# Loading q in long rows, turning it per residue, and keeping TensorE busy during the first loads

## The chip, the cores and the metric

The kernel runs on one NeuronCore of a Trainium2 chip. The metric is the device time of one execution in microseconds (us), as the median of several runs.

## The reference

Two stages follow one another. The first is attention with a decay per head, over 4 batches of 8 heads, 768 positions and 64 dimensions, in blocks of 64 positions with a running state:

```python
for b in range(nb):
    intra = einsum('bhic,bhjc->bhij', qb, kb) * Dmask      # lam ** (i - j) for i >= j
    intra = einsum('bhij,bhjd->bhid', intra, vb)
    inter = einsum('bhid,bhde->bhie', qb * lam_pow, kv_state)
    out[:, :, sl] = intra + inter
    kv_state = lam_block * kv_state + einsum('bhsd,bhse->bhde', kb * rev_pow, vb)
```

The second takes that output as x (4 batches, 768 positions, 512 features) through a mixer over positions and one over features, in float32:

```python
h = relu(x.transpose(0, 2, 1) @ w_tok1) @ w_tok2
u = x + h.transpose(0, 2, 1)
out = u + relu(u @ w_ch1) @ w_ch2
```

## The kernel before

The attention runs over 16 pairs: pair i is one batch and two heads (h = 0, 1), whose 2 x 64 dimensions fill the 128 partitions. The 768 positions stand in six chunks c of 128. Block length in the kernel is the chunk of 128, with the mask and the powers of lam computed on chip for it.

All engines run their instructions in the order in which the program issues them (a manual schedule), so the order of the Python code is the order of each engine's queue. A loop goes over i from -2 to 15, and one turn of it works on several pairs:

- `scores(i + 1)` (L304): for each half g of three chunks, 6 matmuls give k times q into two banks of PSUM; VectorE (DVE) multiplies them by the mask into `a` (L312). `scale_q` (L257, GpSimd, here POOL) multiplies q by powers of lam.
- `outputs(i, g)` (L328 and L338): the weights `a` times v and the scaled q times the state, into `xT`; ScalarE (ACT) copies it to `uT` (L345).
- `state(i + 1)` (L270): k times v per chunk into `kv`, which DVE scans into `sv` with the factors in `keep` (L278). `place`, later, has POOL copy `sv` into `stb` (L291).
- `masks(i + 2)` (L179, for the first four pairs): DVE builds two heads' masks by a scan over the identity.
- the turns of pair i + 2: positions must become the free axis of `kT` and `qT`. For pairs under `NKD` = 8 `turn_k` has TensorE (PE) turn the chunks with the identity into a bank of PSUM, three chunks to a half g, and ACT copies it out (L220, L225). For pairs under `NQ` = 5 `turn_q_rows` does the same for q (L241, L242). Later pairs come by loads of 128-byte rows (`load_dims`, L115) and DVE's 32x32 transposes (L230, L234).
- `turn_back` (L360, L368, L369): the finished `uT` is turned for the mixer and split into a high and a low part.
- `scale_k(i + 2)` (L250 on ACT, L252 on POOL): k times the decay, into `kd`.
- loads, on SyncE's queue (SP): `load_v(i + 3)` (L157), `load_kq(i + 4)` (L137 for k, L140 for q).

Between these steps the code puts work of the mixer over positions: `load_w1` (L407) brings w_tok1 in three parts, and `convert_w1(i)` queues for each part a few steps on DVE, ACT and POOL (L388 to L397, L379, L380), which are taken out one by one during the next turn of the loop. From pair 4 on matmuls with these weights (L456, L493) fill PE beside the attention. After the attention, from about 140 us on, comes the mixer over features.

Before the loop `load_first` loads k of pair 0 from SP and q of pair 0 from ACT, each in four pieces; then v and k, q of the next pairs. `make_identity` builds `ident` on POOL. DVE builds `mask` of the first pair and, by repeated doubling, `lamp` (L198, L201), the powers of lam; POOL copies from it into `keep` for all four pairs of heads (L206). The turns of PE share three banks of PSUM (`bank("sh", ...)`); `xT` has one bank of its own.

As q is loaded before, partition s of the tile holds positions s, s + 128, s + 256 and so on: one piece of 256 bytes for each chunk and head.

Of the kernel before, what the change touches and what calls it, by code (L numbers as in the profile page):

```python
# [9 lines left out]
F32 = mybir.dt.float32  # L10
# [12 lines left out]
def kernel(  # L23
# [23 lines left out]
    nc = tc.nc  # L47
    B, H, S, D = q.shape
# [3 lines left out]
    P = 128  # L52
    NC = S // P
    NH = NC // 2
    NP = H // 2
# [48 lines left out]
    NQ = 5  # L104
    NKD = 8
    loaded = {}
# [3 lines left out]
    def load_dims(to, src, b, p):  # L110
        for h in range(2):
            sv = src[b, 2 * p + h].rearrange("(blk s) (di d) -> di s blk d", s=32, di=2)
            for di in range(2):
# [2 lines left out]
                    out=to[n * 32 : (n + 1) * 32].rearrange("p (blk d) -> p blk d", d=32), in_=sv[di]  # L116
                )

    def load_first():

        kn = kp.tile([P, NC, 2, D], F32, tag="kn", bufs=2, name="kn0")
        qn = kp.tile([P, S], F32, tag="qn", bufs=2, name="qn0")
        for eng, to, src in ((nc.sync, kn, k), (nc.scalar, qn.rearrange("p (c h d) -> p c h d", h=2, d=D), q)):
            for g in range(2):
                for h in range(2):
                    eng.dma_start(
                        out=to[:, 3 * g : 3 * g + 3, h],
                        in_=src[0, h, 3 * g * P : (3 * g + 3) * P].rearrange("(c s) d -> s c d", s=P),
                    )
        loaded[0] = kn, qn  # L130

    def load_kq(i):
        b, p = pairs[i]
        kn = kp.tile([P, NC, 2, D], F32, tag="kn", bufs=2, name=f"kn{i}")
        qn = kp.tile([P, S], F32, tag="qn", bufs=2, name=f"qn{i}")
        for h in range(2):
            nc.sync.dma_start(out=kn[:, :, h], in_=k[b, 2 * p + h].rearrange("(c s) d -> s c d", s=P))  # L137
        if i < NQ:
            for h in range(2):
                nc.sync.dma_start(  # L140
                    out=qn.rearrange("p (c h d) -> p c h d", h=2, d=D)[:, :, h],
                    in_=q[b, 2 * p + h].rearrange("(c s) d -> s c d", s=P),
                )
        else:
            load_dims(qn, q, b, p)
        if i >= NKD:
            kr = kp.tile([P, S], F32, tag="kr", bufs=2, name=f"kr{i}")
            load_dims(kr, k, b, p)
            krs[i] = kr
        loaded[i] = kn, qn  # L150
# [3 lines left out]
    def load_v(i):  # L154
        b, p = pairs[i]
        vns[i] = vn = kp.tile([P, 2, NC, D], F32, tag="vn", bufs=3, name=f"vn{i}")
        nc.sync.dma_start(  # L157
            out=vn.rearrange("p h c d -> p (h c) d"),
            in_=v[b, 2 * p : 2 * p + 2].rearrange("h (c s) d -> s (h c) d", s=P),
        )  # L160
# [7 lines left out]
    keep = ap.tile([P, NP, D, NC - 1], F32, name="keep")  # L168
    lamb = ap.tile([P, H], F32, name="lamb")
    nc.scalar.dma_start(out=lamb, in_=lam[None, :].broadcast_to([P, H]))  # L170
    make_identity(nc, ident)
    load_first()
    load_v(0)
    load_kq(1)
    load_v(1)
# [24 lines left out]
    while n < P:  # L200
# [1 line left out]
            out=lamp[:, :, n : 2 * n], in0=lamp[:, :, 0:n], in1=lamp[:, :, n - 1 : n].broadcast_to([P, NP, n])  # L202
        )
        n *= 2
    for p in range(NP):
        nc.gpsimd.tensor_copy(  # L206
            out=keep[:, p, :, 1:], in_=lamp[:, p, P - 1 : P, None].broadcast_to([P, D, NC - 2])
        )
# [26 lines left out]

    def turn_q_rows(i, g):
        qt = bank("sh", f"qt{i}{g}", 3 * P)
        gs = slice(3 * g * P, (3 * g + 3) * P)
        for c in range(3):
            cs = slice((3 * g + c) * P, (3 * g + c + 1) * P)  # L240
            nc.tensor.transpose(out=qt[:, c * P : (c + 1) * P], in_=loaded[i][1][:, cs], identity=ident)  # L241
        nc.scalar.copy(out=qTs[i][:, gs], in_=qt)  # L242

    def scale_k(i):
        b, p = pairs[i]
        kds[i] = ap.tile([P, 2, NC - 1, D], F32, tag="kd", bufs=1, name=f"kd{i}")
        for h in range(2):
            to, kn, by = kds[i][:, h], loaded[i][0][:, 0 : NC - 1, h], mask[:, 2 * p + h, P - 1 : P]
            if h == 0 or i >= NKD:
                nc.scalar.mul(to, kn, by)  # L250
            else:
                nc.gpsimd.tensor_scalar_mul(to, kn, by)  # L252
# [152 lines left out]
    def load_w1(i):  # L405
        cs = slice(2 * i, 2 * i + 2)
        nc.sync.dma_start(  # L407
            out=words(3).rearrange("p (c f) -> p c f", c=NC)[:, cs],
            in_=w_tok1.bitcast(U32).rearrange("(c s) f -> s c f", s=P)[:, cs],
        )  # L410
# [237 lines left out]
    for i in range(-2, NI):  # L648
        if 0 <= i + 1 < NI:
            scores(i + 1)  # L650
            scale_q(i + 1)
        if i >= 0:
            outputs(i, 0)
        place = state(i + 1) if 0 <= i + 1 < NI else None
        work = [groups.popleft() for _ in range(take.get(i, 0))]
        if i == NI - 1:
            work.pop(0)()
        if i >= 0:
            outputs(i, 1)
            spare.append("xT")  # L660
        if i + 2 < NI and i != LATE:
            turn_q(i + 2)
            if i + 2 >= NKD:
                turn_kr(i + 2)
        if i + 2 < NI:
            if 0 < i + 2 < NP:
                masks(i + 2)
            turns = [(turn_k, 0), (turn_k, 1)] if i + 2 < NKD else []
            if i + 2 < NQ:
                turns += [(turn_q_rows, 0), (turn_q_rows, 1)]  # L670
            if i == -2:
                turns.sort(key=lambda x: x[1])
            for f, g in turns:
                f(i + 2, g)
        if place:
            place()
        later(0 if i == NI - 1 else 1 if work else 2)
        n = early.get(i, len(work) // 4)
        cuts = [0, n, max(n, (3 * len(work) + 1) // 4 if len(work) > 2 else len(work) // 2), len(work)]
        for n in range(3):  # L680
            for f in work[cuts[n] : cuts[n + 1]]:
                f()
                later(2 if len(work) < 3 else 1)
            if n < 2 and i >= 0:
                turn_back(i, n)
                later(1 if work else 2 + n)
            if n == 0 and i + 2 < NI:
                scale_k(i + 2)
        if i == -1:
            load_w1(0)  # L690
        if 0 <= i + 3 < NI and i >= -1:
            load_v(i + 3)
        if i == -1:
            load_w1(1)
        if i + 4 < NI:
            load_kq(i + 4)
        if i == -1:
            load_w1(2)
        if i == 3:
            load_w2()  # L700
        if 0 <= i < 3:
            convert_w1(i)
        if i == 5:
            weights[0] = group_tiles(0, False)
            w3 = words(3)
            load_piece(0, 0, w3[:, 2048:3072])
        if i == 4:
            convert_w2(0)
            convert_w2(1)
        if i == 5:  # L710
            convert_w2(2)
        if i == 6:
            waiting.append(lambda: load_piece(0, 1, w3[:, 1024:2048]))
            steps = narrow_piece(w3[:, 2048:3072], w3[:, 0:512], w3[:, 512:1024])
            turns = [lambda: turn_q(LATE + 2), lambda: turn_kr(LATE + 2)]
            waiting.extend(steps[:1] + 2 * idle + turns[:1] + idle + turns[1:] + idle + steps[1:2] + idle + steps[2:])
        if i == 7:
            steps = narrow_piece(w3[:, 1024:2048], w3[:, 512:1024], w3[:, 2048:2560])
            waiting.extend(steps[:1] + 2 * idle + steps[1:])
            waiting.append(lambda: load_piece(0, 2, w3[:, 2048:3072]))  # L720
        if i == 8:
            waiting.extend(split_c1(weights[0], w3[:, 0:512], w3[:, 512:1024], nc.gpsimd))
        if i == 9:
            waiting.append(lambda: load_piece(0, 3, w3[:, 1024:2048]))
            waiting.extend(narrow_piece(w3[:, 2048:3072], w3[:, 0:512], w3[:, 512:1024]))
            waiting.append(split_c2(weights[0], 2, w3[:, 0:512]))
        if i == 10:
            homes[0] = {"B11": (up, None, 1), "B21": (up, None, 1), "T2": (kp, "kn", 2), "T1": (kp, "qn", 2)}
            homes[0] |= {"B22": (kp, "kr", 2), "T3": (kp, "kT", 2), "T4": (kp, "qT", 2)}
            first = build(0, 0, on_vector=("T1", "T2", "T3", "T4", "B22"))  # L730
            waiting.extend([first["B11"], first["B21"]])
            waiting.extend(narrow_piece(w3[:, 1024:2048], w3[:, 2048:2560], w3[:, 2560:3072]))
            waiting.append(split_c2(weights[0], 3, w3[:, 2048:2560]))
        if i == 11:
            later(99)
        if i == 13:
            for xs in (("t1",), ("t2", "T1.h"), ("T2.h", "T1.l"), ("T2.l", "t3", "t4"), ("T3.h", "T4.h"), ("T3.l", "T4.l")):
                waiting.append(lambda xs=xs: [first[x]() for x in xs])
# [615 lines left out]
```

## Time and profile before

| | |
|---|---|
| median of three runs | 554.91 us (554.79 to 555.17) |
| the profiled execution | 554.8 us, its span 553.0 us |
| PE busy | 542.2 us, 98% of the span |
| DVE, POOL, ACT busy | 437.2, 281.6, 247.4 us |
| first matmul | starts at 4.86 us |
| scores of pair 0 and of pair 1 start | 8.17 and 14.01 us |
| moved by DMA | 66.77 MB in 175,683 packets, 163,600 of them under 512 bytes |

Times inside the profile are counted from the start of the span. PEld is PE's load of the stationary operand, which overlaps its matmuls. In the lines of the order of time the first two numbers are start and duration in us, `x6` is a group of six instructions merged, whose duration runs from the first start to the last end, and the bracket gives how long the engine had been idle and what ended that. `out<-in` names the tiles. A busy PE isn't a PE at its full rate, as the ends of matmuls are modelled.

### The profile page before, as it was taken

Reading aid. Unit: us, or ns where it says so; the run is one execution under the profiler, and the core shown is the slowest. Engines: PE = TensorE matmul, PEld = TensorE weight load, DVE = VectorE, ACT = ScalarE, POOL = GpSimd, SP = SyncE. Lnnn points to the kernel's source line nnn. Section 1 sums busy time; section 2 is a strip of 40 time slices with the busy share of each in tenths; the row PEclk is TensorE's granted clock in tenths of the full one; section 3 lists DMA queues with packets and bytes.
Section 4 is the critical chain, followed back from the end, with each engine's and each line's share of the span. In section 5 each row is a group of like instructions: output and inputs, shape, how many; then the busy total and the mean of one; then the engine's idle time right before and its main releaser. Section 6 shows DMA issues by size and latency. Waiting matters only on the chain.

```text
span 553.0 us, 10803 instructions
## 1 busy us (share of the span) xinstructions
PE 542.2 (98%) x4180; PEld 528.3 (96%) x4180; DVE 437.2 (79%) x657; ACT 247.4 (45%) x499; POOL 281.6 (51%) x256
## 2 busy tenths in 40 slices
PE   6999999999999999999999999999999999999997
PEld 4888998999999999999999999999999999999996
DVE  4787889697786989887878878788777877788894
ACT  3464452335262554343444443443454555445431
POOL 5667453657214564444435444354475656568550
PEclk9999999999999999999999999999999999999999
DMA  9998999998203433361725300024767131220176
GB/s 182 252 208 170 232 186 176 195 196 145 50 2 98 181 114 124 101 223 39 248 78 181 142 1 1 0 30 59 149 137 199 58 116 57 86 105 2 22 155 129
DMA packets 175683, 66.77 MB, mean 121 GB/s; under 512 B 163600, under 2 KB 165904, under 8 KB 175632
## 3 DMA queue, kind: packets, MB, share of 16 engines
q1 hardware_dynamic: 170400, 64.90, 49.0%
q10 hardware_dynamic: 5232, 1.18, 1.0%
q8 instruction: 33, 0.54, 0.4%
q14 instruction: 18, 0.15, 0.1%
HBM read 49.29 MB, written 16.78 MB: 119 GB/s over the span
## 4 chain that ended last, share of the span: by engine, by line
PE 89%; DVE 4%; DMA 3%; ACT 1%; issue 1%; SPq 1%; ACTq 0%; DVEq 0%
PE po L1033 22%; PE pa L807 13%; PE pc L807 9%; PE pb L807 7%; PE pa L1007 7%; PE pc L1007 5%; PE ph L456 5%; PE sc L304 4%; PE pu L493 3%; PE xT L328 3%; PE pd L807 3%; DMA qn<-in_q_dram 3%; PE xT L338 2%; PE pu L476 2%; PE xp L360 1%; PE kv L270 1%
## 5 line engine op out<-in xcount | busy, mean ns | idle before, releaser
L1046 DVE TENSOR_TENSOR uT<-po,uT 128x768 f32<-128x768 f32 x57 | 54.2, 952 | 17.1 <-PE po L1033 16.8
L822 ACT ACTIVATE c<-c 128x384 f32<-128x384 f32 x42 | 22.1, 526 | 59.2 <-DVE c L867 33.5
L291 POOL COPY stb<-sv 64x320 f32<-64x320 f32 x32 | 26.7, 833 | 41.4 <-DVE sv L278 40.5
L1013 DVE TENSOR_TENSOR uT<-pa,uT 128x768 f32<-128x768 f32 x36 | 34.3, 953 | 10.3 <-PE pa L1007 9.6
L328 PE MATMUL xT<-a,vn 128*64 128x128 f32 x384 | 35.7, 277 | 0.0
L824 POOL TENSOR_TENSOR h22l<-c,h22h 128x384 fp32r<-128x384 f32 x14 | 14.4, 1032 | 41.5 <-ACT h22h L823 41.5
L345 ACT COPY uT<-xT 128x384 f32<-128x384 f32 x32 | 15.3, 479 | 44.2 <-PE xT L338 44.1
L1013 DVE TENSOR_TENSOR uT<-pc,uT 128x768 f32<-128x768 f32 x27 | 25.8, 954 | 11.2 <-PE pc L1007 11.2
L312 DVE TENSOR_TENSOR a<-sc,mask 128x768 f32<-128x768 f32 x32 | 29.1, 948 | 4.6 <-PE sc L304 4.5
L338 PE MATMUL xT<-qs,stb 128*64 128x128 f32 x320 | 31.3, 273 | 0.0
L380 POOL TENSOR_TENSOR c1l<-cs,c1h 128x512 fp32r<-128x512 f32 x15 | 19.3, 1298 | 23.1 <-ACT c1h L379 23.1
L456 PE MATMUL ph<-xhi,w1h 128*128 128x256 f32 x96 | 28.2, 293 | 0.7 <-DVE sv L278 0.4
L1033 PE MATMUL po<-h12h,c 128*128 128x384 f32 x112 | 28.7, 337 | 0.0
L1033 PE MATMUL po<-h11h,c 128*128 128x384 f32 x112 | 28.6, 336 | 0.0
L1033 PE MATMUL po<-h22h,c 128*128 128x384 f32 x112 | 28.6, 336 | 0.0
L1033 PE MATMUL po<-h21h,c 128*128 128x384 f32 x112 | 28.6, 336 | 0.0
L304 PE MATMUL sc<-qT,kT 64*128 64x128 f32 x384 | 27.1, 290 | 0.3 <-ACT qT L242 0.2
L304 PEld LDWEIGHTS sc<-qT,kT 64*128 64x128 f32 x384 | 23.9, 196 | 3.5 <-issue 1.7
L456 PE MATMUL ph<-xhi,w1l 128*128 128x256 f32 x96 | 27.1, 282 | 0.0
L456 PE MATMUL ph<-xlo,w1h 128*128 128x256 f32 x96 | 27.1, 282 | 0.0
L369 DVE TENSOR_TENSOR xlo<-xp,xhi 128x384 fp32r<-128x384 f32 x32 | 17.7, 553 | 11.0 <-ACT xhi L368 10.8
L257 POOL TENSOR_TENSOR qs<-qT,lamp 128x640 f32<-128x640 f32 x16 | 25.5, 1592 | 0.3
(397 smaller groups left out, 1944.0 us busy)
## 6 DMA issues: line engine op xcount, KB each, us to landing
raw<-in_moe_w_ch_dram SPq DMA_DIRECT2D x20, 512.0 KB, 3.7
vn<-in_v_dram SPq DMA_DIRECT2D x16, 384.0 KB, 5.3
kn<-in_k_dram SPq DMA_DIRECT2D x30, 192.0 KB, 5.4
out_dram<-y SPq DMA_DIRECT2D x104, 48.0 KB, 1.9
qn<-in_q_dram SPq DMA_DIRECT2D x44, 96.0 KB, 4.0
kr<-in_k_dram SPq DMA_DIRECT2D x32, 96.0 KB, 2.7
dc1h<-c1h SPq DMA_DIRECT2D x4, 768.0 KB, 5.3
dc1l<-c1l SPq DMA_DIRECT2D x4, 768.0 KB, 6.7
```

Of the source, the lines that this page charges most:

```text
L257: nc.gpsimd.tensor_mul(out=qss[i], in0=qTs[i][:, P:].rearrange("p (c i) -> p c i", i=P), in1=lamp[:, p, None, :].broadcast_to([P, NC - 1, P]),
L291: nc.gpsimd.tensor_copy(out=st[r, :, h, :], in_=sv[r].rearrange("p (e c) -> p c e", c=NC - 1))
L304: nc.tensor.matmul(out=sc[h][:, c * P : (c + 1) * P], lhsT=kTs[i][r, cs], rhs=qTs[i][r, cs], start=True, stop=True,)
L312: nc.vector.tensor_mul(out=a, in0=pair.rearrange("p h (c i) -> p h c i", i=P), in1=mask[:, 2 * p : 2 * p + 2, None, :].broadcast_to([P, 2, ...
L328: nc.tensor.matmul(out=xT[h * D : (h + 1) * D, cs], lhsT=vns[i][:, h, c, :], rhs=weights_of[i, g, h][:, cg, :], start=(cg == 0), stop=False,)
L338: nc.tensor.matmul(out=xT[h * D : (h + 1) * D, cs], lhsT=st[:, c - 1, h, :], rhs=qss[i][:, c - 1, :], start=False, stop=(cg == 2),)
L456: nc.tensor.matmul(out=ph, lhsT=w[:, c, fs], rhs=x[:, c], start=(i == 0), stop=(i == 3 * NC - 1))
L807: nc.tensor.matmul(out=to, lhsT=w[:, t], rhs=x[:, t], start=(start and i == 0), stop=(i == 5), skip_group_check=not start,)
L1007: nc.tensor.matmul(out=pair[x][:, t], lhsT=w[:, t], rhs=h, start=(start and i == 0), stop=(i == 2), skip_group_check=not start,)
L1013: nc.vector.tensor_add(out=ub, in0=pair[x], in1=ub)
L1033: nc.tensor.matmul(out=to, lhsT=w[:, jj, t * P : (t + 1) * P], rhs=h, start=(i == 0), stop=(i == 3 * JG - 1))
L1046: nc.vector.tensor_add(out=ub, in0=po, in1=ub)
```

## The change

Five edits come together.

1. q of pairs 0 to 4 is loaded so that partition s holds the six positions 6s to 6s + 5 of a head, 1536 bytes in one piece. A pair's q is one load on SP (two on ACT for pair 0).
2. `turn_q_rows` takes residue c (positions 6s + c, for all s) in place of chunk c: for each residue and head one matmul with the identity as moving operand, 64 columns wide, into one half of the partitions. Three residues make a half g, and the copy out of PSUM writes every sixth column of `qT`. The copy of the second half is DVE's for pairs 0 and 1; the others are ACT's.
3. PE turns the identity 15 times into an unread bank before the first loads have landed, and four times after the first turn of k. A one-column copy on ACT stands ahead of its first real one. The order of the turns is k, q, q, k for pair 0 and q, q, k, k for pair 1; pair 1's q is loaded ahead of its k.
4. The second and third part of w1 are loaded one and two turns of the loop later, behind that turn's v, k and q.
5. POOL fills `keep` for one pair of heads in each of the first four turns of the loop, behind `scale_k`, in place of all four ahead of it.

```diff
+    def load_rows(eng, qn, i, hs):
+        b, p = pairs[i]
+        eng.dma_start(
+            out=qn.rearrange("p (h x) -> p h x", h=2)[:, hs],
+            in_=q[b, 2 * p : 2 * p + 2].rearrange("h (s c) d -> s h (c d)", c=NC)[:, hs],
+        )
...
+        for h in range(2):
+            load_rows(nc.scalar, qn, 0, slice(h, h + 1))
         loaded[0] = kn, qn
...
+        if i == 1:
+            load_rows(nc.sync, qn, i, slice(0, 2))
         for h in range(2):
             nc.sync.dma_start(out=kn[:, :, h], in_=k[b, 2 * p + h].rearrange("(c s) d -> s c d", s=P))
...
+        if 1 < i < NQ:
+            load_rows(nc.sync, qn, i, slice(0, 2))
+        elif i >= NQ:
             load_dims(qn, q, b, p)
...
+    primed = ap.tile([P, 1], F32, name="primed")
     make_identity(nc, ident)
+    idle_bank = bank("xT", "idle", P)
+
+    def spin(n):
+        for _ in range(n):
+            nc.tensor.transpose(out=idle_bank, in_=ident, identity=ident)
+
+    spin(15)
     load_first()
+    nc.scalar.copy(out=primed, in_=ident[:, 0:1])
...
-    for p in range(NP):
+    def keeps(p):
...
     def turn_q_rows(i, g):
         qt = bank("sh", f"qt{i}{g}", 3 * P)
-        gs = slice(3 * g * P, (3 * g + 3) * P)
+        qn = loaded[i][1].rearrange("p (h c d) -> p h c d", h=2, d=D)
         for c in range(3):
-            cs = slice((3 * g + c) * P, (3 * g + c + 1) * P)
-            nc.tensor.transpose(out=qt[:, c * P : (c + 1) * P], in_=loaded[i][1][:, cs], identity=ident)
-        nc.scalar.copy(out=qTs[i][:, gs], in_=qt)
+            for h in range(2):
+                nc.tensor.matmul(
+                    out=qt[h * D : (h + 1) * D, c * P : (c + 1) * P],
+                    lhsT=qn[:, h, 3 * g + c],
+                    rhs=ident,
+                    start=(c == 0),
+                    stop=(c == 2),
+                )
+        copy = nc.vector.tensor_copy if i < 2 and g else nc.scalar.copy
+        copy(
+            out=qTs[i].rearrange("p (s c) -> p c s", c=NC)[:, 3 * g : 3 * g + 3],
+            in_=qt.rearrange("p (c s) -> p c s", c=3),
+        )
...
             if i == -2:
-                turns.sort(key=lambda x: x[1])
+                turns = [turns[n] for n in (0, 2, 3, 1)]
+            if i == -1:
+                turns = turns[2:] + turns[:2]
             for f, g in turns:
                 f(i + 2, g)
+                if i == -2 and f is turn_k and g == 0:
+                    spin(4)
...
                 scale_k(i + 2)
+                if i + 2 < NP:
+                    keeps(i + 2)
         if i == -1:
             load_w1(0)
         if 0 <= i + 3 < NI and i >= -1:
             load_v(i + 3)
-        if i == -1:
-            load_w1(1)
         if i + 4 < NI:
             load_kq(i + 4)
-        if i == -1:
-            load_w1(2)
+        if -1 <= i < 1:
+            load_w1(i + 2)
```

More of the change, by code (lines that the diff above doesn't have):

```diff
@@ L122, in load_first @@
         qn = kp.tile([P, S], F32, tag="qn", bufs=2, name="qn0")
[L123 to L129, printed above, removed]
+        for g in range(2):
+            for h in range(2):
+                nc.sync.dma_start(
+                    out=kn[:, 3 * g : 3 * g + 3, h],
+                    in_=k[0, h, 3 * g * P : (3 * g + 3) * P].rearrange("(c s) d -> s c d", s=P),
+                )
+        for h in range(2):
+            load_rows(nc.scalar, qn, 0, slice(h, h + 1))
         loaded[0] = kn, qn
@@ L135, in load_kq @@
         qn = kp.tile([P, S], F32, tag="qn", bufs=2, name=f"qn{i}")
+        if i == 1:
+            load_rows(nc.sync, qn, i, slice(0, 2))
         for h in range(2):
             nc.sync.dma_start(out=kn[:, :, h], in_=k[b, 2 * p + h].rearrange("(c s) d -> s c d", s=P))
[L138 to L144, printed above, removed]
+        if 1 < i < NQ:
+            load_rows(nc.sync, qn, i, slice(0, 2))
+        elif i >= NQ:
             load_dims(qn, q, b, p)
@@ L237, in turn_q_rows @@
         qt = bank("sh", f"qt{i}{g}", 3 * P)
-        gs = slice(3 * g * P, (3 * g + 3) * P)
+        qn = loaded[i][1].rearrange("p (h c d) -> p h c d", h=2, d=D)
         for c in range(3):
-            cs = slice((3 * g + c) * P, (3 * g + c + 1) * P)
-            nc.tensor.transpose(out=qt[:, c * P : (c + 1) * P], in_=loaded[i][1][:, cs], identity=ident)
-        nc.scalar.copy(out=qTs[i][:, gs], in_=qt)
+            for h in range(2):
+                nc.tensor.matmul(
[9 more added lines that the diff above has]
+            in_=qt.rearrange("p (c s) -> p c s", c=3),
+        )
     def scale_k(i):
```

## The prediction, made before the changed kernel ran

> **What bounds the kernel now.** I read the page first (busy shares), then a table of stretches, then the chain and the order of time for the first 15 us, because all edits sit in the load and turn of pairs 0 to 4.
>
> ```profile
> span 553.0 us, 10803 instructions
> PE 542.2 (98%) x4180; PEld 528.3 (96%) x4180; DVE 437.2 (79%) x657; ACT 247.4 (45%) x499; POOL 281.6 (51%) x256
> ```
>
> The table of stretches (busy us of PE, PEld, DVE, ACT, POOL, then granted clock, DMA share, GB/s):
>
> ```profile
> 0.00:10.00 10.00, 4.80 (x28) 3.98 (x30) 2.73 (x12) 3.66 (x6) 5.77 (x15) 1.00 0.91 168
> 10.00:20.00 10.00, 9.51 (x144) 8.38 (x140) 7.47 (x10) 3.87 (x9) 6.87 (x7) 1.00 1.23 242
> 20.00:30.00 10.00, 9.75 (x140) 8.35 (x138) 7.29 (x11) 6.46 (x16) 5.45 (x6) 1.00 1.06 248
> 30.00:40.00 10.00, 9.99 (x169) 9.10 (x169) 9.33 (x14) 6.05 (x14) 7.04 (x6) 1.00 1.07 188
> ```
>
> PE is busy in 542.2 of 553.0 us. It idles 5.2 us in the first 10, 0.49 and 0.25 us in the next two stretches, then hardly at all. So the change can win only in the start and in a few stalls before 30 us; whatever comes later moves as a block. The DMA share is at or over 0.91 all through: loads are a queue without gaps.
>
> The order of time of the start, the row that sets each step:
>
> ```profile
> 0.99 0.29 POOL masks.py:199 TENSOR_SCALAR_AFFINE_SELECT ident<-ident 128x128 f32<-128x128 f32 x1
> 4.86 0.87 PE L220 MATMUL kt<-ident,kn 128*128 128x128 f32 x3 [4.86 <-DMA kn<-in_k_dram]
> 5.16 1.85 DVE L201 TENSOR_TENSOR lamp<-lamp 128x4 f32<-128x4 f32 x7
> 6.07 0.87 PE L241 MATMUL qt<-ident,qn 128*128 128x128 f32 x3 [0.34 <-DMA qn<-in_q_dram]
> 8.17 2.93 PE L304 MATMUL sc<-qT,kT 64*128 64x128 f32 x24
> 9.87 0.96 DVE L312 TENSOR_TENSOR a<-sc,mask 128x768 f32<-128x768 f32 x1 [2.86 <-PE sc L304]
> 11.15 0.96 DVE L312 TENSOR_TENSOR a<-sc,mask 128x768 f32<-128x768 f32 x1 [0.32 <-PE sc L304]
> 11.77 0.88 PE L220 MATMUL kt<-ident,kn 128*128 128x128 f32 x6
> 12.03 0.81 DVE L278 TENSOR_TENSOR_SCAN sv<-keep,kv 128x320 f32<-128x320 f32 x1
> 12.75 1.24 DVE L179 TENSOR_TENSOR_SCAN mask<-lamb,ident 128x128 f32<-128x128 f32 x2
> 12.89 0.88 PE L241 MATMUL qt<-ident,qn 128*128 128x128 f32 x6 [0.25 <-DVE sv L278]
> 13.47 0.86 ACT L242 COPY qT<-qt 128x384 f32<-128x384 f32 x2 [0.26 <-PE qt L241]
> 14.01 1.61 PE L304 MATMUL sc<-qT,kT 64*128 64x128 f32 x24 [0.24 <-ACT qT L242]
> 14.99 1.82 DVE L312 TENSOR_TENSOR a<-sc,mask 128x768 f32<-128x768 f32 x2 [1.00 <-PE sc L304]
> ```
>
> Two readings. First, pair 0's 24 score matmuls take 2.93 us and pair 1's take 1.61: PE runs slowly until about 11 us, though the granted clock in the table says 1.00. One transposing matmul shows it too (one line, before 8 us and from 11.8 us):
>
> ```profile
> L220 PE MATMUL kt<-ident,kn x6: 421/421/445, 4.9 to 7.2; 128*128 128x128 f32 x6
> ...
> L220 PE MATMUL kt<-ident,kn x24: 272/273/332, 11.8 to 33.7; 128*128 128x128 f32 x24
> ```
>
> Second, 14.01 (pair 1's scores) is the mark I use: after it PE runs nearly gapless, so a shift there is a shift of the end.
>
> **The change part by part.**
>
> *Spin.* 15 turns of the identity can start at 1.28 us (0.99 + 0.29). Cold turns follow each other 0.21 us apart (three in 0.87, the last lasting 0.42), so they fill 1.3 to 4.5 us, while PE waits for k until 4.86: no cost. The four behind the first k turn cost 0.85 us cold, 0.45 warm; they cover the wait that ended at 6.07. If q is there sooner, they are a delay. Gain if PE is warm when scores begin: 2.93 − 1.61 = 1.3 us, and less for the turns.
>
> *Loads of q.* Rows of 1536 bytes in place of 256. The trace has no such packet; the nearest stretches bound it:
>
> ```profile
> 6.00:8.00 2.00, 1.93 (x9) 1.65 (x9) 0.94 (x3) 1.11 (x3) 0.84 (x3) 1.00 1.34 226
> 20.00:22.00 2.00, 2.00 (x25) 1.60 (x25) 0.56 (x1) 2.00 (x6) 1.90 (x3) 1.00 1.03 303
> ```
>
> 226 GB/s is 256-byte rows alone, 303 a mixture with 2048-byte rows of w1. A pair's q (393 KB) takes 1.74 us at the first, 1.30 at the second; I take 1.3, as 1536 is nearest to 2048. Five pairs save 2.2 us of DMA time, one third of it before pair 1. But pair 1's k now comes behind its q: 1.18 MB of k and v at 226 plus 0.79 MB of q at 226 to 303 is 7.8 to 8.7 us. I let it start at 2 us and allow 1 us to land, estimates from the first k (192 KB, landed by 4.86): 11 to 11.9 us. Covered, below, by DVE; without that cover its turn and copy (0.3 + 0.5) put pair 1's scores at 12.7. ACT issues two DMAs fewer; vn0's issue has fewer ahead of it. w1's parts 1 and 2 go one and two iterations later, behind v and k, q: nobody waits on SP for them, and the first use of each part stays an iteration off; zero, or a DVE stall if part 2 lands after about 41 us.
>
> *The copies, and their queue.* Each turned half now writes every sixth column, so pair i's first score matmul needs both q copies, where it needed one. For pairs 0 and 1 the second copy is DVE's, in program order. For pair 0 it stands behind the lamp products, which end at 5.16 + 1.85 = 7.01. A contiguous DVE read of such a bank is here:
>
> ```profile
> 21.31 0.56 DVE L369 TENSOR_TENSOR xlo<-xp,xhi 128x384 fp32r<-128x384 f32 x1 [1.77 <-ACT xhi L368]
> 27.45 0.90 DVE L391 SCALAR_TENSOR_TENSOR uT<-uT,uT 128x512 uint32<-128x512 uint32 x1
> 30.22 0.69 DVE L397 SCALAR_TENSOR_TENSOR uT<-uT 128x512 uint32<-128x512 uint32 x1
> 28.20 0.69 ACT L387 ACTIVATE uT<-uT 128x512 f32<-128x512 f32 x1
> 30.94 0.62 ACT L379 CAST w1h<-uT 128x512 fp32r<-128x512 f32 x1 [0.85 <-DVE uT L397]
> ```
>
> L391 and L387 read every second word, L397 and L379 every word: strides cost DVE 1.3 times, ACT 1.1. A write 24 bytes apart is in no row. Bounds: DVE 0.55 to 0.9 us, ACT 0.48 to 0.8 (the DVE ratio doubled). I take 0.7 and 0.53, from each engine's own pair of rows.
>
> Pair 0: k's turn at 4.9 to 5.1 us, done by 5.7; spin to 6.3; twelve q matmuls (half warm, 0.8 to 1.4 us) to 7.4; DVE's copy 0.7: scores start at S = 8.1 (7.6 at best, which lamp sets; 9.0 cold). So S stays where it was, 8.17.
>
> Pair 1: DVE must do both a, sv and mask before its copy. Warm: a at S + 0.98 (14.01 to 14.99), 1.82 for both, 0.72 for sv (12.03 to 12.75), 1.24 for mask, 0.7 for the copy: S + 5.5 = 13.6, against 14.01. The 1.3 us that a warm PE wins mostly turn into a wait in DVE's queue; behind it on PE stand pair 1's scores and everything after. Gain 0.4 us.
>
> *Pairs 2 to 4.* Twelve 64-column matmuls replace six turns; eight of the former took 0.66 us with the tail, six of the latter 0.88, so no cost in work. But PE changes its tile shape twice more per pair:
>
> ```profile
> 17.93 0.39 PE L338 MATMUL xT<-qs,stb 128*64 128x128 f32 x4
> 18.14 0.39 PE L328 MATMUL xT<-a,vn 128*64 128x128 f32 x4
> 18.36 0.39 PE L338 MATMUL xT<-qs,stb 128*64 128x128 f32 x4
> 18.68 0.55 PE L220 MATMUL kt<-ident,kn 128*128 128x128 f32 x3
> 19.27 0.86 ACT L225 COPY kT<-kt 128x384 f32<-128x384 f32 x2
> 20.03 0.87 ACT L242 COPY qT<-qt 128x384 f32<-128x384 f32 x2
> 21.04 0.30 PEld L304 LDWEIGHTS sc<-qT,kT 64*128 64x128 f32 x4 [0.17 <-issue]
> 26.84 0.84 PE L241 MATMUL qt<-ident,qn 128*128 128x128 f32 x6 [0.25 <-DMA qn<-in_q_dram]
> ```
>
> Four matmuls of one shape follow in 0.22 us, the change to 128x128 in 0.32: 0.1 us each, 0.2 a pair. Pair 3 wins back its wait for q (0.25, to 0.4 with what PEld waited). Sum over three pairs: −0.6 + 0.4, and some of the changes hide under ACT: −0.1 us. ACT's two copies end at 20.90, 0.14 before the scores at 21.04; the change of shape adds 0.2 of cover, so 0.1 more for both is free.
>
> *The rest.* ACT's early table load, the keep copies spread over POOL behind kd, mean no wait on the path: POOL's kd of pair 0 can start earlier, and kv needs it only after the scores. Zero; if keep were late, sv would wait 0.4 us.
>
> **Sum.** 0.4 − 0.1 = 0.3 us off. The profiled execution took 554.80 us (span 553.0 and 1.8 around it), 0.11 under the median of 554.91. So 554.5 for its like, and on the median 554.6; I put 554.5.
>
> **Rivals.** *Faster: the queue doesn't bind.* If pair 0's copies are ready at 7.6 and the DVE copies cost 0.55, pair 1's scores start at 7.6 + 5.35 = 12.95, 1.05 us early, and both q stalls go (0.4, and an estimated 0.15 at pair 4), less 0.2 for shapes: 1.4 us, 553.5. For: all loads are earlier. Against: k's landing and lamp each stand close to it. It decides from scores at or before 13.0. Chance 0.36.
>
> *Slower: the turns don't warm PE.* In the trace PE turned almost steadily from 6.07, and ran cold until the score matmuls had gone on for 2.8 us. If turns of the identity count for nothing, spin(4) is a delay: S = 8.7, a at S + 1.70, second a at S + 2.98, mask's end at S + 5.8 (8.17 to 13.99), copy 0.7: 15.2, 1.2 us late: 556.1. It decides if pair 0's scores last over 2.5 us. The Trainium skill, "TensorE: Matmul & The Clock Gate", Part 4, states that rule: transpose-mode work does not count as PE activity for the clock gate. The trace doesn't exclude it, since 1.5 us of steady turning is short. Chance 0.12.
>
> *Slower: the strided copies are dear.* At 0.8 us each on ACT and 0.9 on DVE, pair 1's scores come at 13.8 (0.2 early); two copies add 0.64 in each of pairs 2 to 4, of which 0.1 to 0.3 is covered: 1.5 late in all, net 1.3: 556.2. It decides from 0.65 us a copy on ACT. The Trainium skill, "SBUF — State Buffer", Door 1, says a 16-byte line wants two hits and each crossing pays; it would put every write of these copies on a new line. No run here shows a write of that kind. Chance 0.10.
>
> **How the numbers follow.** My forecast, no change, has 0.42. 0.2% (1.1 us) is about what a measurement of this kernel can tell from none: 553.8 to 556.0. Faster 0.36, same 0.42, slower 0.22. Alone its range is 553.8 to 555.6; with the fast case and most of both slow ones, 553.0 to 556.3.
>
> **What would show it.** Right: pair 0's 24 scores near 1.6 us, starting near 8.1; DVE's second q copy of pair 1 right behind mask; PE idle some 1 us before pair 1's scores at 13.6; no wait for q at pair 3; 0.3 us between unlike shapes. Wrong, if pair 1's scores start before 13.0 (the queue is no bound), if those of pair 0 still last 2.9 us, or if an ACT copy of q takes 0.65 us or more.

## The result, and the profile after

The changed kernel takes 558.08 us (six runs, 557.95 to 560.02) where the kernel before takes 554.93 beside it (six runs): a ratio of 1.0063, interval 1.0053 to 1.0074. It is slower by about 3 us; the prediction said 554.5, and its range ended at 556.3. The profiled execution is the longest of the six, 560.02 us (the one before: 554.80), so its span shows 5.1 us of loss, of which some 2 us are not in the other five runs (557.95 to 558.21). Both parts are traced below.

The page of the changed kernel, span and busy time:

```profile
span 558.1 us, 11016 instructions
PE 548.7 (98%) x4289; PEld 534.4 (96%) x4289; DVE 438.4 (79%) x659; ACT 249.9 (45%) x498; POOL 281.6 (50%) x256
```

PE is busy 6.5 us longer and has 109 instructions more. Nineteen of these are turns of the identity; the other 90 are work that the prediction did not count. The table of stretches (columns as before: busy time of PE, PEld, DVE, ACT, POOL, granted clock, DMA share, GB/s):

```profile
0.00:10.00 10.00, 7.68 (x48) 6.81 (x49) 2.71 (x12) 2.82 (x4) 4.46 (x11) 1.00 0.83 192
10.00:20.00 10.00, 8.37 (x147) 7.48 (x147) 7.01 (x9) 3.60 (x7) 6.09 (x6) 1.00 1.04 237
20.00:30.00 10.00, 9.86 (x153) 8.53 (x149) 6.76 (x11) 5.20 (x11) 5.58 (x7) 1.00 0.92 235
30.00:40.00 10.00, 9.86 (x152) 8.53 (x151) 8.33 (x12) 7.10 (x15) 6.29 (x7) 1.00 0.81 185
```

From 10 to 20 us PE is busy 1.1 us less than before; the start has become a wait. From 20 us on it is as full as it was, yet falls further behind: there the loss is work, not waiting. The order of time, the start and then pair 2 (start, duration, instruction, and in brackets how long the engine idled ahead of it and what ended that):

```profile
1.34 3.46 PE L183 MATMUL idle<-ident 128*128 128x128 f32 x15 [1.34 <-POOL ident masks.py:199]
...
5.59 1.85 DVE L216 TENSOR_TENSOR lamp<-lamp 128x4 f32<-128x4 f32 x7
...
5.78 0.87 PE L235 MATMUL kt<-ident,kn 128*128 128x128 f32 x3 [0.97 <-DMA kn<-in_k_dram]
6.44 1.06 PE L183 MATMUL idle<-ident 128*128 128x128 f32 x4
7.43 2.41 PE L256 MATMUL qt<-ident,qn 128*64 128x128 f32 x24
...
9.90 0.84 DVE L264 COPY qT<-qt 128x384 f32<-128x384 f32 x1 [2.46 <-PE qt L256]
...
10.88 1.61 PE L329 MATMUL sc<-qT,kT 64*128 64x128 f32 x24 [0.56 <-ACT kT L240]
...
13.05 1.48 PE L256 MATMUL qt<-ident,qn 128*64 128x128 f32 x24
...
14.32 1.25 DVE L194 TENSOR_TENSOR_SCAN mask<-lamb,ident 128x128 f32<-128x128 f32 x2
...
15.50 0.81 DVE L264 COPY qT<-qt 128x384 f32<-128x384 f32 x1
...
16.45 1.61 PE L329 MATMUL sc<-qT,kT 64*128 64x128 f32 x24 [1.07 <-ACT kd L275]
...
21.93 1.53 PE L256 MATMUL qt<-ident,qn 128*64 128x128 f32 x24
...
22.91 1.55 ACT L264 COPY qT<-qt 128x384 f32<-128x384 f32 x2 [0.34 <-PE qt L256]
23.40 0.98 PE L385 MATMUL xp<-ident,uT 128*128 128x128 f32 x6
...
24.52 1.42 PEld L329 LDWEIGHTS sc<-qT,kT 64*128 64x128 f32 x24 [0.38 <-ACT qT L264]
```

Pair 0's scores start at 10.88 in place of 8.17, pair 1's at 16.45 in place of 14.01. The last bracket of pair 1 names ACT's `kd`; the wait is for DVE's copy, which ends at 16.31, 0.14 us before the scores. In every run with two strided copies pair 1's scores start 0.14 to 0.16 us after that copy ends, and where the copy is no longer needed first (`flat_copy` below) they don't wait for it.

What the turn of q costs is clearest in the groups of the tile `qt` (count, then ns min/median/max, first and last start). The kernel before:

```profile
L241 PE MATMUL qt<-ident,qn x30: 272/273/448, 6.1 to 34.6; 128*128 128x128 f32 x30
L242 ACT COPY qT<-qt x10: 479/482/490, 7.0 to 35.0; 128x384 f32<-128x384 f32 x10
```

and the changed one:

```profile
L256 PE MATMUL qt<-ident,qn x120: 272/273/476, 7.4 to 39.4; 128*64 128x128 f32 x120
L264 ACT COPY qT<-qt x8: 857/886/939, 9.0 to 39.7; 128x384 f32<-128x384 f32 x8
L264 DVE COPY qT<-qt x2: 809/822/836, 9.9 to 15.5; 128x384 f32<-128x384 f32 x2
```

Five pairs have 30 turns in the code before, and 30 rows. The changed code has 60 matmul calls in their place, and 120 rows. One plain float32 call is two instructions, one transposing call is one. That is the 90. And the copies take 0.86 to 0.94 us on ACT, not 0.48.

The starts of the pairs' scores in the profiled executions, with the medians, give one table for all that follows (us; the median of the kernel before in the same session: 554.79 for the first four rows behind "after", 554.64 for the next four, 554.70 for the last four). The profiled executions of `after`, `one_turn`, `flat_copy`, `one_turn_flat` and `long_rows` took 0.8 to 1.9 us more than their medians, so their starts lie later than in most runs.

| kernel | pair 0 | 1 | 2 | 3 | 4 | 5 | median | ratio to before, interval |
|---|---|---|---|---|---|---|---|---|
| before | 8.17 | 14.01 | 21.04 | 28.46 | 35.64 | 42.09 | 554.93 | |
| after | 10.88 | 16.45 | 24.52 | 32.62 | 40.71 | 47.07 | 558.08 | 1.0063 (1.0053 to 1.0074) |
| after_again | 11.01 | 16.61 | 24.67 | 32.76 | 40.85 | 47.20 | 559.78 | 1.0084 (1.0067 to 1.0100) |
| one_turn | 9.58 | 15.15 | 22.77 | 30.43 | 38.09 | 44.58 | 557.42 | 1.0042 (1.0029 to 1.0056) |
| flat_copy | 10.51 | 15.22 | 22.96 | 30.71 | 38.46 | 44.88 | 556.11 | 1.0028 (1.0016 to 1.0041) |
| one_turn_flat | 9.14 | 14.07 | 21.11 | 28.14 | 35.22 | 41.77 | 554.03 | 0.9987 (0.9978 to 0.9996) |
| no_spin | 10.28 | 15.97 | 24.02 | 32.09 | 40.18 | 46.53 | 559.26 | 1.0083 (1.0070 to 1.0097) |
| spin_21 | 9.45 | 15.03 | 23.09 | 31.19 | 39.27 | 45.62 | 558.22 | 1.0065 (1.0051 to 1.0078) |
| long_rows | 8.59 | 14.49 | 21.52 | 28.56 | 35.63 | 42.20 | 554.29 | 0.9991 (0.9982 to 1.0001) |
| late_w1_spin | 7.58 | 13.67 | 20.70 | 27.73 | 34.81 | 41.39 | 554.27 | 0.9996 (0.9987 to 1.0004) |
| rows_two | 9.64 | 15.21 | 22.24 | 29.27 | 36.34 | 42.93 | 555.70 | 1.0016 (1.0007 to 1.0025) |
| spin_alone | 7.57 | 13.65 | 20.91 | 28.29 | 35.48 | 41.92 | 555.14 | 1.0007 (0.9998 to 1.0016) |
| late_w1 | 8.01 | 13.74 | 20.78 | 27.81 | 34.88 | 41.45 | 554.37 | 0.9996 (0.9988 to 1.0005) |
| one_long | 8.31 | 13.93 | 20.96 | 28.00 | 35.06 | 41.91 | 554.20 | 0.9990 (0.9981 to 0.9999) |

After pair 5 all moves as a block: the changed kernel is 4.98 us late there and 5.1 at the end of the span. So 2.44 us are lost before pair 1's scores, and 2.6 between pair 1 and pair 4. On the median the loss is 3.15 us; if pairs 2 to 4 cost the shorter executions the same 2.6, some 0.5 is left for their start (an estimate, as none of them was profiled).

### The profile page after: what moved, and what is told of

Its sections match the earlier page's. It is cut to its first block, busy times and chain, and to the rows that moved or that the text cites. A ratio compares the mean times of both kernels' runs of the same rounds, so it can differ in the third digit from the quotient of the medians.

```text
span 558.1 us, 11016 instructions
## 1 busy us (share of the span) xinstructions
PE 548.7 (98%) x4289; PEld 534.4 (96%) x4289; DVE 438.4 (79%) x659; ACT 249.9 (45%) x498; POOL 281.6 (50%) x256
## 4 chain that ended last, share of the span: by engine, by line
PE 89%; DVE 5%; ACT 2%; DMA 1%; issue 1%; SPq 1%; DVEq 0%; ACTq 0%
PE po L1062 21%; PE pa L836 12%; PE pc L836 9%; PE pb L836 7%; PE pa L1036 7%; PE pc L1036 5%; PE ph L481 5%; PE sc L329 3%; PE pu L518 3%; PE xT L353 3%; PE pd L836 3%; PE xT L363 2%; PE pu L501 1%; PE kv L295 1%; PE qt L256 1%; PE xp L385 1%
## 5 line engine op out<-in xcount | busy, mean ns | idle before, releaser
L329 PE MATMUL sc<-qT,kT 64*128 64x128 f32 x384 | 25.7, 280 | 2.2 <-ACT kd L275 1.1
```

The costliest lines, as they stand in the source:

```text
L329: nc.tensor.matmul(out=sc[h][:, c * P : (c + 1) * P], lhsT=kTs[i][r, cs], rhs=qTs[i][r, cs], start=True, stop=True,)
```

## The experiments

The theory from the two traces had two parts. *Work*: in pairs 2 to 4 the doubled matmuls and the strided copies cost some 1 us a pair, whatever the loads do. *Start*: pair 0 is late because k lands later and the q turn runs while PE is slow; DVE's queue then passes that on to pair 1. The rivals: the loads themselves, by contention, set the pace of all pairs; the turns of the identity only delay; the queue on DVE alone makes the loss.

### The changed kernel again, and its two halves taken back

`after_again` is the changed kernel, unchanged, beside the next three.

> The changed kernel once more, for a second profile of it: the first one's span (558.1 us) is 1.9 us over those of its other runs (556.2 to 556.4). If the difference lies in when TensorE becomes fast, this profile's pair 0 turns and scores come up to 1.9 us earlier and everything from pair 2 on is the same; if it lies later, the starts of pair 0's and pair 1's scores agree with 10.88 and 16.45 us.

It took 559.78 us, with one run of four at 558.26 and three at 559.73 to 560.05. Its profiled execution is of the long kind, like the first:

```profile
5.50 0.88 PE L235 MATMUL kt<-ident,kn 128*128 128x128 f32 x3 [0.69 <-DMA kn<-in_k_dram]
...
7.15 2.83 PE L256 MATMUL qt<-ident,qn 128*64 128x128 f32 x24
...
11.01 1.61 PE L329 MATMUL sc<-qT,kT 64*128 64x128 f32 x24 [0.37 <-DVE qT L264]
```

k comes 0.28 us earlier than in the first trace and the q turn takes 0.42 us longer: it is cold over its whole length. The kernel runs at about 558.0 or about 559.9 us.

`one_turn` turns two residues of one head at once with a transposing matmul, half as many calls; its q is therefore in another order.

```diff
-            for h in range(2):
-                nc.tensor.matmul(
-                    out=qt[h * D : (h + 1) * D, c * P : (c + 1) * P],
-                    lhsT=qn[:, h, 3 * g + c],
-                    rhs=ident,
-                    start=(c == 0),
-                    stop=(c == 2),
-                )
+            nc.tensor.transpose(
+                out=qt[:, c * P : (c + 1) * P],
+                in_=loaded[i][1][:, (3 * g + c) * P : (3 * g + c + 1) * P],
+                identity=ident,
+            )
```

> The changed kernel with each residue turned by one 128-column transposing matmul on 128 neighbouring columns in place of two plain 64-column matmuls (so two residues of one head are turned together, and the scores are of other columns). Theory of the passes (a plain float32 matmul runs as two instructions, 24 a pair where six turned before, 1.5 us against 0.85): 2.5 us less than the changed kernel, about 555.5. Rival, the strided copies bound pairs 2 to 4: at most 1.2 us less, all of it before pair 1's scores, since ACT's two copies (1.55 us) still end last.

Pair 3, in its trace:

```profile
28.15 0.82 PE L255 MATMUL qt<-ident,qn 128*128 128x128 f32 x6
28.77 1.60 ACT L261 COPY qT<-qt 128x384 f32<-128x384 f32 x2
...
29.73 0.55 PE L382 MATMUL xp<-ident,uT 128*128 128x128 f32 x3 [0.23 <-ACT qT L261]
30.43 1.61 PE L326 MATMUL sc<-qT,kT 64*128 64x128 f32 x24 [0.15 <-ACT qT L261]
```

It takes 557.42 us, far from the 555.5 of the theory. The turn is back at 0.82 us, 0.71 less than the 1.53 above, but the period from pair to pair falls from 8.10 to 7.66 only. PE now waits for ACT's strided copies: 0.23 ahead of `xp`, 0.15 ahead of the scores. In the start pair 0's scores come 1.30 us earlier than in the first trace.

`flat_copy` keeps the twelve matmuls and leaves out the change of order in the copy (q stays in the order of its residues).

```diff
-            out=qTs[i].rearrange("p (s c) -> p c s", c=NC)[:, 3 * g : 3 * g + 3],
-            in_=qt.rearrange("p (c s) -> p c s", c=3),
+            out=qTs[i][:, 3 * g * P : (3 * g + 3) * P],
+            in_=qt,
```

> The changed kernel with both copies of q writing neighbouring columns (q stays in residue order in qT, so the scores are of other columns). Theory of the passes: little, 0.3 to 1.0 us less, as TensorE's 24 matmuls a pair stay; pair 1's scores 0.35 us earlier by DVE's shorter copy. Rival, the strided copies (0.86 us on ACT, 0.84 on DVE, where 0.48 stood) carry the loss: 2.5 to 3 us less, 555.3.

```profile
28.45 1.53 PE L256 MATMUL qt<-ident,qn 128*64 128x128 f32 x24
29.42 1.08 ACT L264 COPY qT<-qt 128x384 f32<-128x384 f32 x2 [0.34 <-PE qt L256]
...
29.91 0.88 PE L385 MATMUL xp<-ident,uT 128*128 128x128 f32 x6
30.71 1.61 PE L329 MATMUL sc<-qT,kT 64*128 64x128 f32 x24
```

Its 556.11 us lie between the two expectations. ACT's two copies take 1.08 us (the second waits for PE), no wait is left on PE, and the period is 7.75: pure work, 0.7 more than the 7.05 of `one_turn_flat` below, for the doubled turn and its two changes of shape. Pair 1's scores come at S + 4.71 in place of S + 5.57, where S is the start of pair 0's: the first score matmul needs the first copy alone again, and DVE's second copy (15.13, 0.53 us) ends after the scores have begun at 15.22.

`one_turn_flat` has both edits.

> Both edits: one transposing matmul of 128 columns a residue, and flat copies. Passes and copies together explain the loss of pairs 2 to 4 (0.9 to 1.1 us a pair): 4.3 us less than the changed kernel, 553.8, and from pair 1's scores on as before the change. Rival, the loss is made at the start (k landing 0.9 us later, the spin behind it): 1.5 to 2 us remain over the kernel before, 556.5.

554.03 us, 0.9987 of before, and a period of 7.03 to 7.08. Alone the two edits win 0.44 and 0.35 us a pair, together 1.05: with one gone the other binds, PE's work or ACT's copies. From pair 1's scores to pair 4's it needs 21.15 us, the changed kernel 24.26 and the kernel before 21.63. So turn and copies cost 3.1 us there, and the loads, which are all still in this version, win 0.5 of it back: the 2.6 is the difference. As the pace of pairs 2 to 4 the rival by contention falls. What these loads could bring, with a turn and a copy that cost as little as before, is 0.1%.

### The start: the spin and the rows

`no_spin` takes the 19 turns of the identity out of the changed kernel.

```diff
-    spin(15)
...
-                if i == -2 and f is turn_k and g == 0:
-                    spin(4)
```

> The changed kernel without the idle turns (neither the 15 nor the 4). If turns of the identity make TensorE fast: it stays slow until 9 to 12 us, pair 0's scores last up to 2.9 us, and the time is 0.5 to 1.5 us over the changed kernel's. Rival, turns don't count and the four are a plain delay: pair 0's scores start 0.9 us earlier than at 10.9 to 11.0, and the time is 0.5 to 1 us less.

`spin_21` lengthens them, so that no gap is left before k.

```diff
-    spin(15)
+    spin(21)
```

> The changed kernel with 21 idle turns in place of 15, so that they last until k lands (about 5.8 us) without the gap of 0.7 to 1.0 us. If turns count, and the gap is what makes some executions 1.8 us longer than others: TensorE is fast by 8.3 us, pair 0's q turn lasts under 2.2 us, and all runs lie near 558.0. Rival, turns don't count: fast from 9.3 us or later as before, and runs at 558 and 560.

The starts of the two, first without turns:

```profile
5.39 0.87 PE L228 MATMUL kt<-ident,kn 128*128 128x128 f32 x3 [5.39 <-DMA kn<-in_k_dram]
6.19 3.07 PE L249 MATMUL qt<-ident,qn 128*64 128x128 f32 x24
```

then with 21:

```profile
3.74 2.34 PE L183 MATMUL idle<-ident 128*128 128x128 f32 x10
...
5.88 0.65 PE L235 MATMUL kt<-ident,kn 128*128 128x128 f32 x3
...
6.89 1.53 PE L256 MATMUL qt<-ident,qn 128*64 128x128 f32 x24
...
9.45 1.61 PE L329 MATMUL sc<-qT,kT 64*128 64x128 f32 x24 [0.55 <-ACT kT L240]
```

With 21 turns PE is fast from the first k turn on (0.65 us for three where cold takes 0.87), and the q turn takes 1.53 in place of 3.07 us; nothing but transposing matmuls had run by then. All runs lie at 557.94 to 558.41. Without any turns they lie at 558.95 to 559.46. With 15 turns, and a gap of 0.7 to 1.0 us behind them, PE became fast late in the q turn (2.41 us) or behind it (2.83) in the two profiled executions of the changed kernel, and the runs lie at 558.0 or 559.9. That the 558.0 runs are those in which PE was fast in time fits the narrow spread with 21 turns, but none of them was profiled: argued, not shown. The turns of the identity are worth about 1 us when they reach up to k, so the rival that they only delay falls. With the gap it describes what the traces show: pair 0's scores start at 10.88 and 11.01 us with 15 turns and the four behind k, at 10.28 without any.

`rows_two` puts the long rows of pairs 2 to 4 back to 256-byte pieces, with their old turn and copy; pairs 0 and 1 stay as changed, with 21 turns of the identity.

> The changed kernel with 21 idle turns, and with long rows, plain matmuls and strided copies for pairs 0 and 1 alone; pairs 2 to 4 load and turn q as before the change. Theory (pairs 2 to 4 lose about 1 us each in their turn of q): pair 1's scores at 15.0 us as with 21 turns, then 7.0 to 7.2 us from pair to pair in place of 8.1, and 555.5. Rival, the loss comes with the loads or their order: the time stays over 557.

555.70 us. It is 2.5 us below `spin_21`, and its period is 7.03 to 7.07: the cost of pairs 2 to 4 by the other way. What is left, 1.0 us over before (1.0016, interval 1.0007 to 1.0025), is the start: pair 1's scores at 15.21.

`long_rows` is the kernel before with only q's loads of pairs 0 to 4 in long rows (`load_rows` for q, the old turns and copies, so that q comes in another order).

> The kernel before with only the loads of q changed to 1536-byte rows (turned as before, so columns stand in another order and the scores are of other columns). If the long packets of q take DMA time from the first k: pair 0's first k turn starts at 5.5 instead of 4.86 us, pair 3's wait for q (0.4 us) is gone, and the time is within 0.6 us of the kernel before, 554.8. Rival, the loads are a plain gain: first turn at 4.9 us and 1 us less, 553.8.

```profile
5.66 0.87 PE L224 MATMUL kt<-ident,kn 128*128 128x128 f32 x3 [5.66 <-DMA kn<-in_k_dram]
...
8.59 2.94 PE L308 MATMUL sc<-qT,kT 64*128 64x128 f32 x24
...
14.49 1.61 PE L308 MATMUL sc<-qT,kT 64*128 64x128 f32 x24 [0.24 <-ACT qT L246]
```

Between 3 and 4.5 us the two DMA queues moved (packets, MB, share of 16 engines; q1 is SP's, with k, q10 ACT's, with q), first in the kernel before, then in `long_rows`:

```profile
q1 hardware_dynamic: 870, 0.21, 63.8%
q10 hardware_dynamic: 690, 0.16, 48.5%
...
q10 hardware_dynamic: 174, 0.17, 39.5%
q1 hardware_dynamic: 407, 0.10, 29.9%
```

q gets as many bytes as in the kernel before (0.17 against 0.16 MB) and k half as many (0.10 against 0.21), though SP issues k's loads at the same time in both. The rows alone move k's first turn from 4.86 to 5.66, and pair 1's scores 0.48 us back; pair 3's wait for q, gone, gives that back (28.56 against 28.46, 35.63 against 35.64). The sum is 554.29 against 554.64, an interval that touches 1. Over all profiled executions k's first turn starts at 4.61 to 5.05 where pair 0's q comes in 256-byte pieces (five kernels) and at 5.39 to 5.78 where it comes in long rows (seven; in two more the 21 turns of the identity last until then, and it starts at 5.88).

### The edits that need neither the new turn nor the new copy

`spin_alone` is the kernel before with the 15 turns of the identity ahead of the loop, `late_w1` with the second and third part of w1 loaded later, `late_w1_spin` with both.

```diff
+    spin(15)
...
-        if i == -1:
-            load_w1(1)
...
-        if i == -1:
-            load_w1(2)
+        if -1 <= i < 1:
+            load_w1(i + 2)
```

> The kernel before with 15 idle turns and with w1's second and third part loaded later; q is loaded and turned as before. If q's landing bounds pair 1 (it lands at about 12.7 us) and pair 3's wait for q goes: 0.4 to 0.7 us less than before, 554.2. Rival, a fast TensorE at the start is worth its full 1.3 us: 553.2. Rival, no gain: 554.8.

> The kernel before with 15 idle turns and nothing else. If q's landing holds pair 1 (it waited 0.95 us for it with spin and late w1), and w1's early parts hold pair 3's q: pair 0's scores end 1.9 us earlier, pair 1's start at 13.7, pair 3 waits for q 0.3 us longer, and the time is within 0.4 us of the kernel before. Rival, the idle turns are the whole gain of the run with late w1: 554.3 here too.

> The kernel before with w1's second and third part loaded one and two turns of the loop later, and nothing else. Pair 3 no longer waits for q (0.4 us) and pair 4 hardly (0.15): 0.3 to 0.5 us less than before, 554.3. Rival, the wait is given back to VectorE's chain before pair 6: no difference.

They took 554.27, 555.14 and 554.37 us; none is told from 1 by its interval. In the trace of `spin_alone` the scores of pair 0 are fast at 7.57, and the loads take it back:

```profile
7.57 1.61 PE L311 MATMUL sc<-qT,kT 64*128 64x128 f32 x24
...
10.78 0.84 PE L227 MATMUL kt<-ident,kn 128*128 128x128 f32 x6 [0.61 <-DMA kn<-in_k_dram]
...
12.56 0.84 PE L248 MATMUL qt<-ident,qn 128*128 128x128 f32 x6 [0.94 <-DMA qn<-in_q_dram]
...
13.65 1.61 PE L311 MATMUL sc<-qT,kT 64*128 64x128 f32 x24 [0.24 <-ACT qT L249]
```

A warm PE is 1.9 us ahead by the end of pair 0's scores (9.18 against 11.10), and then waits 1.55 us for k and q of pair 1. The bound of the start has moved from PE to the loads.

`one_long` answers that wait: `late_w1_spin`, and pair 1's q alone in one long-row load ahead of its k, with the new turn and copies for that pair, which come ahead of its masks on DVE.

```diff
+        if i == 1:
+            load_rows(nc.sync, qn, i, slice(0, 2))
...
+            if i == -1:
+                turns = turns[2:] + turns[:2]
...
+            if i == -1:
+                masks(1)
```

> The kernel before with 15 idle turns, late w1, and pair 1's q alone in long rows, loaded ahead of its k, turned by plain matmuls and copied by ACT and DVE, whose mask for pair 1 stands behind its copy. In the run with spin and late w1 TensorE idled 0.6 and 0.95 us there, which covers the double passes: pair 1's scores at 13.1 to 13.3 instead of 13.67, 0.4 us less than that run, 553.8. Rival, strided copies and passes eat it: 554.3 or more.

```profile
5.05 0.88 PE L238 MATMUL kt<-ident,kn 128*128 128x128 f32 x3 [0.25 <-DMA kn<-in_k_dram]
...
8.31 2.53 PE L339 MATMUL sc<-qT,kT 64*128 64x128 f32 x24
11.39 1.48 PE L266 MATMUL qt<-ident,qn 128*64 128x128 f32 x24
...
13.93 1.61 PE L339 MATMUL sc<-qT,kT 64*128 64x128 f32 x24 [0.19 <-ACT kT L243]
```

554.20 us, 0.9990 (0.9981 to 0.9999): half a us better than before. `late_w1_spin` without the long row took 554.27 (0.9996), so a gain by the row itself isn't shown. Beside `one_turn_flat`, which leaves the order of q undone, it is the one version that its interval puts below 1, and only just. The wait for pair 1's q is gone. The profiled execution did not reach the 13.1 to 13.3 hoped for pair 1's scores: PE had waited 0.25 us for k and was still cold, and pair 0's scores took 2.53 us. That this wait kept it cold is argued; the last section has the figures.

## Why the prediction was wrong

**The step that failed is *Pairs 2 to 4*.** It counted twelve matmuls in place of six turns and read "eight of the former took 0.66" as eight calls. They are eight rows, that is four calls:

```profile
15.54 0.66 PE L328 MATMUL xT<-a,vn 128*64 128x128 f32 x8
```

L328 has 384 rows over 16 pairs, 24 a pair, where the code has 12 calls (six chunks, two heads). Read rightly, the same row gives the cost that came: 24 rows at its spacing of 0.056 us ((0.66 − 0.27) / 7) with a tail of 0.27 are 1.55 us, measured 1.53, against 0.82 to 0.88 for six turns. "No cost in work" was 0.7 us a pair, the two changes of shape included (7.75 against 7.05). With ACT's strided copies the period rose by 1.05, and with pair 3's and pair 4's waits won back the three pairs lost 2.6 us (16.45 to 40.71 against 14.01 to 35.64), where the prediction won 0.1. Of the 3.6 us between the predicted 554.5 and the median of 558.08 these are 2.7; the rest is the start. The same misreading stands in pair 0's "twelve q matmuls (half warm, 0.8 to 1.4 us)": they take 1.53 fast and 3.07 cold.

**The copies** were the mis-sized term beside it: 0.53 on ACT and 0.7 on DVE taken, 0.86 to 0.94 and 0.82 measured. The upper bounds, 0.8 and 0.9, were nearer; the rows of strided reads were no guide to strided writes. Of the extra 0.8 us on ACT for two copies, 0.35 a pair reached the period of the changed kernel (8.10 against 7.75), and 0.61 where the turn was short (7.66 against 7.05). The slow rival on the copies had this price nearly right, but gave 556.2 since it too left the matmuls' work at zero.

**The loads and the spin**: k was to start at 4.9 to 5.1 and came at 5.78; that q's long rows take this time from it was no term of the sum (`long_rows`: 5.66). S was to be 8.1 and is 10.88, by the terms of the prediction: k 0.8 later, spin(4) 0.3 longer as it ran cold, the q turn 2.41 in place of 1.1, the DVE copy 0.14 and the wait for `kT` behind it 0.14. Warm throughout (`spin_21`) S is 9.45, still 1.35 too late: k 0.9 later, the doubled turn 0.4 longer, DVE's copy and the wait behind it 0.3 longer, and the four turns 0.3 shorter.

**Right**: the queue on DVE. Pair 1's scores were to stand at S + 5.5; they stand at S + 5.57, S + 5.60 and S + 5.58 in three traces, with DVE's copy right behind `mask` and PE idle 1.07 us before them. Right too: no wait for q at pair 3, two shape changes of 0.1 us each, and no cost of the moved `keep`. Pair 1's k behind its q cost nothing, for the reason given.

**The rivals**: the faster one needed scores at or before 13.0, and the best version with the new turn had 13.93. The one by which turns do not warm PE would show 24 scores over 2.5 us; they took 1.61. That alone decides nothing, as pair 0's scores come so late that they take 1.74 without any turns of the identity (`no_spin`); `spin_21` decides, with PE fast and only transposing matmuls behind it. The rule of the Trainium skill, "TensorE: Matmul & The Clock Gate", Part 4, that transpose-mode work does not count for the clock gate, is not borne out here: the trace's clock record for TensorE rises at 6.19 us in `spin_21`, at 5.23 in `spin_alone` and at 6.53 in `late_w1_spin`, against 10.99 in the kernel before, with nothing but transposing matmuls before it.

## What to carry to other kernels

Before pricing a replaced instruction, count the rows of the old and of a like new form against the calls in the code: here one plain float32 matmul is two rows, one transposing matmul one, so a turn by plain matmuls into half the partitions costs four times as many instructions. When a layout change moves the stride from a load to a copy, price the strided write from a write, and ask whether the reader now needs all of the copies before its first instruction. Two edits that each win a third may win everything together, so test them both ways.

## What the runs showed of the hardware

- Copies of 128x384 float32 from PSUM with a write step of 24 bytes took 0.84 to 0.95 us on ACT and 0.81 to 0.86 on DVE; to contiguous words 0.48 to 0.52 and 0.53 to 0.56.
- The trace holds a record of TensorE's granted clock, which begins where the clock rises; ahead of that the tables print 1.00, although the rows show PE slow there. From rise to fall it lasts 542.72, 546.13 or 549.55 us in the fourteen traces, that is 159, 160 or 161 times 3.4133, so rise and fall stand on a grid of 3.413 us. The rise is at 6.19 and 6.58 us in the two traces with 21 turns of the identity, at 9.29 and 10.34 in the two traces of the changed kernel with 15, at 10.58 with none. In the 3.413 us ahead of each rise PE's matmul rows cover 92 to 100% of the time, in the 3.413 us before those 84% at most (`one_long`). That a gap of under 1 us in the turns cost a whole step fits these figures, but isn't shown: the grid stands elsewhere against the start in each execution.
- A load in long rows on one queue held back one in 256-byte pieces on another: k's first turn starts at 4.61 to 5.05 us without it, at 5.39 to 5.78 with it.
